# Keys and values as five tokens on each of 116 partitions: a fused cosformer attention and SwiGLU kernel

## The chip, the cores and the metric

The kernel runs on one core of one Trainium2 chip. The metric is device time in microseconds (us). Engines are called PE (TensorE; PEld is its weight load), DVE (VectorE), ACT (ScalarE), POOL (GpSimd) and SP (SyncE). SP computes nothing: it issues transfers, in its program's order. ACT and POOL issue transfers too. 16 DMA engines of the core carry them out.

## The reference

There are 8 batches, 8 heads, 576 tokens and a head size of 64. First linear attention, then a gated feed-forward layer on the 4,608 token rows of 512 numbers:

```python
r = np.maximum(x, 0.0)
phi(x) = np.concatenate([r * c, r * s], axis=-1)   # c, s: cos and sin of pi/2 * pos / S
kv = einsum('bhsf,bhsd->bhfd', phi(k), v);  z = sum(phi(k), axis=2)
num = einsum('bhsf,bhfd->bhsd', phi(q), kv)
den = einsum('bhsf,bhf->bhs', phi(q), z)[..., None] + 1e-06
x = num / den                                      # then the heads side by side: (4608, 512)
xn = x / sqrt(mean(x * x) + 1e-06) * rms_g
out = (silu(xn @ w_gate) * (xn @ w_val)) @ w_out   # 512 -> 1536 -> 512
```

All inputs and the output are float32. The sum over tokens in kv and z takes the tokens in any order, as long as k, v and the table of angles agree.

## The kernel before, in words

**Layout.** k and v of a batch are loaded into a tile `raw` of 128 partitions (line 77). Even heads lie on partitions 0 to 63, odd heads on 64 to 127; each partition holds nine consecutive tokens of its head (`kv_rows`, line 65; NC = 9), so one row piece is 9 x 64 x 4 = 2,304 bytes and a load has 128 x 4 pieces. `k_phi` (255) makes phi for one of the nine token slots `c`, all heads, one half (cos on DVE, sin on ACT): an instruction of 128 x 256 elements. `v_cast` (303) turns v to bf16 with a column of ones beside it, which gives z with kv. `kvz_pe` (312) multiplies: for each head pair, slot and half, a product over 64 rows, 72 in all per batch. For batch 0 the z sums (`z0_pe`, 324) and the kv sums (`kv0_pe`, 333) are made apart, since its v (`vv0`, cast by the load itself) comes later than k.

**After that, per batch:** the copy of the sums (`kvz_evac`, 343), eight products of 128 rows for each of four 128-token tiles (`nd_pe`, 347), the division (`nd_post`, 383), the norm (`x_sq`, `x_norm`), and a transpose that fills `xnT`, the moving operand of the feed-forward layer. Batches 0 and 1 are transposed by PE, later ones by transposes on the DMA engines issued from SP (`q_tr_dma` 278, `q_tails_tr_dma` 286, `x_tr_dma` 429).

**Blocks.** The feed-forward layer goes by blocks of 512 tokens, in the order 0, 1, 2, 3, 4, 5, 6, 8, 7; block 8 is the 64 last tokens of each batch ("tails"). A block has 12 steps of gate and value products (`gval_step`, 716) and four output tiles (`out_step`, 725; numbered 12 to 15). Attention work of the next batch is put between these steps by hand, in `slots`: `at(blk, n, where, f, ...)` (624) runs `f` in step n of block blk, "pe" before its matmuls, "pre" before the evaluation of its results, "post" after it. Every engine carries out its instructions in this written order.

**The order that the steps below touch.** For a batch nb from 2 on, processed in block b = nb - 1: k phi and v casts in steps 12 to 15 of block b - 1; q phi with its transposes in (b-1, 14), (b-1, 15), (b, 0), (b, 1); `kvz_pe` in step 2; `nd_pe` in steps 4, 6, 8, 10, the xn transposes one step later each. Block nb needs all of xnT before its first matmul. Loads of batch b + 2 are issued from SP in block b: k in step 0, v in step 3, q in step 6 (in block 1: 0, 5, 8). So SP's queue in a block reads: q transpose, k, q transpose, tail transpose, v, xn transpose, q, three xn transposes, then the output stores. The five `raw` buffers are a ring.

**Opening.** SP loads batch 0's k in two pieces (tokens 0 to 4 and 5 to 8 of each partition, lines 115, 116); ACT loads the gain `g4` (118); POOL issues q and v of batch 0, then the weights, batch 1's k and so on (157 to 175, 540 to 602). While k is on its way PE runs ten filler matmuls (505), DVE makes the table of angles (208 to 220) and splits the gain into three bf16 parts (`g_parts`, 183), which PE spreads over the partitions (`g_spread`, 196). Then phi of the nine slots (506 to 519), q, kv, and the first block in quarters as its inputs come (589 to 619).

**End.** The last output tile of block 7 is computed in two halves of 256 columns (728 to 734), so that the first is copied and stored while the second is computed.

Of the kernel before, what the change touches and what calls it, by code (L numbers as in the profile page):

```python
# [9 lines left out]
FP32 = mybir.dt.float32  # L10
# [7 lines left out]
def kernel(  # L18
# [18 lines left out]
    NC = S // 64  # L37
# [27 lines left out]
    def kv_rows(src, b, hps):  # L65
        return src[b, 2 * hps[0] : 2 * hps[1], :, :].rearrange(
            "(hp hh) (s c) d -> (hh s) hp (c d)", hh=2, c=NC
        )

# [5 lines left out]
    def raw_tile(which, b):  # L75
        if (which, b) not in raw:
            t = ring.tile([P, HP * NC * D], FP32, name="raw", tag="raw")
            raw[(which, b)] = t
        return raw[(which, b)]

    def raw_kv(which, b):
        return raw_tile(which, b)[:, :].rearrange("p (hp e) -> p hp e", hp=HP)
# [4 lines left out]
    def load_kv(which, b, hps=(0, HP), eng=nc.sync):  # L87
        src = k if which == "k" else v
        return eng.dma_start(
            out=raw_kv(which, b)[:, hps[0] : hps[1], :], in_=kv_rows(src, b, hps)  # L90
        )

    def load_q(b, js=(0, 4), eng=nc.sync):
        return eng.dma_start(
            out=raw_q(b)[:, :, js[0] * D : js[1] * D],
            in_=q_rows(b)[:, :, js[0] * D : js[1] * D],
        )
# [11 lines left out]
    def load_k_tokens(b, c0, c1):  # L109
        return nc.sync.dma_start(  # L110
            out=raw_kv("k", b)[:, :, c0 * D : c1 * D],
            in_=kv_rows(k, b, (0, HP))[:, :, c0 * D : c1 * D],
        )

    load_k_tokens(0, 0, 5)
    load_k_tokens(0, 5, NC)
    g4 = one.tile([4, P], FP32, name="g4")
    nc.scalar.dma_start(out=g4[:, :], in_=moe_rms_g.rearrange("(t p) -> t p", p=P))


    idx_i = one.tile([P, 14], mybir.dt.int32, name="idx_i")
    G.iota(idx_i[:, 0:9], pattern=[[1, 9]], base=0, channel_multiplier=9)
    G.iota(idx_i[:, 9:13], pattern=[[1, 4]], base=0, channel_multiplier=4)
    G.iota(idx_i[:, 13:14], pattern=[[0, 1]], base=512, channel_multiplier=1)
# [31 lines left out]
    vv0 = one.tile([P, HP, NC * D], BF16, name="vv0")  # L156
    load_q(0, (0, 2), G)
    for hp in range(0, HP, 2):
        G.dma_start(out=vv0[:, hp : hp + 2, :], in_=kv_rows(v, 0, (hp, hp + 2)))
    load_q(0, (2, 4), G)  # L160
    for n in range(0, NNT - 4, 4):
        load_w(wg, moe_w_gate, n, n + 4)
        load_w(wv, moe_w_val, n, n + 4)
# [13 lines left out]

    g3 = one.tile([4, 3, P], BF16, name="g3")
    gres = one.tile([4, 2, P], FP32, name="gres")
    sel = one.tile([4, NDT, P], BF16, name="sel")  # L180
    gb = one.tile([P, DM], FP32, name="gb")

    def g_parts():
        V.tensor_copy(
            out=sel[:, :, :], in_=ident[0:4, 0:4].unsqueeze(2).to_broadcast([4, NDT, P])
        )
        rest = g4
        for i in range(3):
            V.tensor_copy(out=g3[:, i, :], in_=rest[:, :])
            if i < 2:  # L190
                V.tensor_tensor(
                    out=gres[:, i, :], in0=rest[:, :], in1=g3[:, i, :], op=ALU.subtract
                )
                rest = gres[:, i, :]

    def g_spread(bank):
# [8 lines left out]
    fidx = one.tile([P, 14], FP32, name="fidx")  # L205
    th = one.tile([P, 28], FP32, name="th")
    tab = one.tile([P, 28], FP32, name="tab")
    V.tensor_copy(out=fidx[:, :], in_=idx_i[:, :])
    V.tensor_scalar(
        out=th[:, 0:14], in0=fidx[:, :], scalar1=ang, scalar2=None, op0=ALU.mult  # L210
    )
    for c0, c1, less in ((0, 9, 576.0), (13, 14, 64.0)):
        V.tensor_scalar(
            out=th[64:128, c0:c1], in0=fidx[64:128, c0:c1], scalar1=-less, scalar2=ang,
            op0=ALU.add, op1=ALU.mult,
        )
    V.tensor_scalar(
        out=th[:, 14:28], in0=th[:, 0:14], scalar1=math.pi / 2.0, scalar2=math.pi,
        op0=ALU.add, op1=ALU.min,
    )  # L220
    A.activation(out=tab[:, :], in_=th[:, :], func=AF.Sin)

# [3 lines left out]
    def cos_of(c):  # L226
        return tab[:, 14 + c : 15 + c]

    kp = one.tile([P, NC, HP, F], BF16, name="kp")
    vv = one.tile([P, HP, NC, E], BF16, name="vv")  # L230
# [24 lines left out]
    def k_phi(eng, b, c, part, hps=(0, HP)):  # L255
        o = slice(0, D) if part == 0 else slice(D, F)
        f = cos_of if part == 0 else sin_of
        src = raw_kv("k", b)[:, hps[0] : hps[1], c * D : (c + 1) * D]
        phi(eng, kp[:, c, hps[0] : hps[1], o], src, f(c))
# [8 lines left out]
    def q_phi(eng, b, j, part):  # L268
        o = slice(0, D) if part == 0 else slice(D, F)
        f = cos_of if part == 0 else sin_of  # L270
        phi(eng, qp_of((b, j))[:, :, o], raw_q(b)[:, :, j * D : (j + 1) * D], f(9 + j))

    def q_tails_phi(eng, pair, part):
        o = slice(0, D) if part == 0 else slice(D, F)
        f = cos_of if part == 0 else sin_of
        phi(eng, qp_of(("t", pair))[:, :, o], rqt[pair][:, :, :], f(13))
# [26 lines left out]
    def v_cast(eng, b, hps=(0, HP)):  # L303
        copy(
            eng, vv[:, hps[0] : hps[1], :, 0:D],
            raw_kv("v", b)[:, hps[0] : hps[1], :].rearrange("p hp (c d) -> p hp c d", d=D),
        )
# [4 lines left out]
    def kvz_pe(b, hps=range(HP)):  # L312
        for hp in hps:
            for c in range(NC):
                for g in range(2):
                    lo, hi = 64 * g, 64 * g + 64
                    nc.tensor.matmul(  # L317
                        heads[:, g, hp, :], lhsT=kp[lo:hi, c, hp, :], rhs=vv[lo:hi, hp, c, :],
                        start=(c == 0), stop=(c == NC - 1),
                    )  # L320
# [3 lines left out]
    def z0_pe(c):  # L324
        for hp in range(HP):
            for g in range(2):
                lo, hi = 64 * g, 64 * g + 64
                nc.tensor.matmul(
                    heads[:, g, hp, D:E], lhsT=kp[lo:hi, c, hp, :], rhs=ones[lo:hi, :],
                    start=(c == 0 and hp == 0), stop=False, skip_group_check=True,  # L330
                )

    def kv0_pe(hp):
        for c in range(NC):
            for g in range(2):
                lo, hi = 64 * g, 64 * g + 64
                nc.tensor.matmul(
                    heads[:, g, hp, 0:D], lhsT=kp[lo:hi, c, hp, :],
                    rhs=vv0[lo:hi, hp, c * D : (c + 1) * D],
                    start=False, stop=(hp == HP - 1 and c == NC - 1), skip_group_check=True,  # L340
                )
# [148 lines left out]
    def filler_k(c):  # L490
        for _ in range(2):
            nc.tensor.matmul(  # L492
                psC[1][:, 0 : HP * D], lhsT=warm[:, 0:P], rhs=kp[:, c, :, 0:D],
                start=True, stop=True,
            )
# [8 lines left out]
    g_parts()  # L504
    filler(10, psC[1])
    for c in range(NC):
        k_phi(V, 0, c, 0)
        if c < 7:
            k_phi(A, 0, c, 1)
        filler_k(c)  # L510
        if c == 3:
            g_spread(psC[0])
        if c == 6:
            for i in range(6):
                z0_pe(i)
    k_phi(V, 0, 7, 1)
    k_phi(V, 0, 8, 1)
    for i in range(6, NC):
        z0_pe(i)
# [111 lines left out]
    KCS = ((0, 1, 2), (3, 4), (5, 6), (7, 8))  # L631
    for c in range(NC):
        at(0, 4 + c // 3, "post", k_phi, V, 1, c, 0)
        at(0, 4 + c // 3, "post", k_phi, A, 1, c, 1)
# [6 lines left out]
    at(0, 8, "post", load_kv, "k", 2, (0, HP), G)  # L641
    at(0, 9, "post", v_cast, G, 1, (0, 2))
    at(0, 10, "pre", v_cast, V, 1, (2, 4))
    at(0, 10, "post", load_kv, "v", 2, (0, HP), G)
# [23 lines left out]
    for nb in range(2, B):  # L668
# [7 lines left out]
        for i in range(2):  # L676
            vb, vn = ((0, 15), (1, 0))[i] if first else (b - 1, 13 + 2 * i)
            at(vb, vn, "post", v_cast, V, nb, (2 * i, 2 * i + 2))
# [46 lines left out]
    def out_step(blk, j):  # L725
        n = 12 + j
        run(blk, n, "pe")
        if blk == last_blk and j == 3:
            for i, bank in enumerate((psC[1], psG[0])):
                cols = (256 * i, 256 * i + 256)  # L730
                for m in range(NNT):
                    out_mm(j, m, bank, cols)
                out_store(A if i == 0 else V, blk, j, bank, cols)
            return
        bank = psC[j % 2]
        for m in range(NNT):
            if m == NNT // 2:
                run(blk, n, "mid")
            out_mm(j, m, bank)
        run(blk, n, "pre")  # L740
        out_store(A, blk, j, bank)
        run(blk, n, "post")
# [40 lines left out]
```

## Time and profile before

| | |
|---|---|
| median of 3 runs | 326.97 us (326.74 to 327.19) |
| the profiled execution, device time | 327.27 us |
| its span, first to last instruction | 325.5 us |
| granted PE clock | 1.000 |
| PE, DVE, ACT, POOL busy | 97%, 56%, 52%, 12% of the span |
| HBM read, written | 37.75 MB, 9.44 MB |
| DMA queue of SP: packets, MB, share of 16 engines | 65,952, 39.73, 52.7% |
| DMA queue of POOL | 7,216, 13.17, 16.3% |
| k, v, q loads from SP: size, median time from issue to landing | 1152, 1152, 1024 KB: 7.2, 6.6, 8.5 us |
| batch 0's k, two pieces | 640 KB 5.0 us, 512 KB 6.0 us |
| q transposes, xn transposes | 24 and 24: 3.6 and 3.0 us to landing |
| phi of k: DVE, ACT, mean of one | 355 ns x74, 501 ns x70 |
| k-v products of 64 rows by 65 columns | 504 (seven batches) |

The page's first part gives each engine's busy share; its second cuts the span into 40 slices of 8.1 us, with busy tenths, and the bytes moved per second; its third lists the DMA queues. The chain is the work that ended last, followed back. A timeline row reads: start, duration, engine, line, operation, what is written and read, count, and in brackets the idle time ahead with its releaser; for SP it is the time of issue. A window row gives, for a stretch, busy times, the clock, the DMA engines' share and GB/s.

### The profile page before, as it was taken

The page shows a single profiled execution, that of the slowest core. Times are in us where ns is not written, and L with a number is a line of the kernel's source. Part 1 is how long each engine was busy: PE and PEld are TensorE (multiplying, and loading weights), DVE is VectorE, ACT ScalarE, POOL GpSimd, SP SyncE. Part 2 cuts the span into 40 slices and gives each one's busy share as a digit, 9 for nine tenths or more (in the row PEclk, how much of TensorE's full clock was granted, in tenths as well). Part 3 has the DMA queues.
Part 4 walks back from the last instruction along what each step waited for, and adds up shares of the span by engine and source line. Part 5 has one row for each costly group of instructions (what it writes and reads, how often), then busy time and mean ns, then how long its engine had stood idle before and what let it go on. Part 6 is the DMA issues. An engine that isn't in the chain of part 4 may idle for free.

```text
span 325.5 us, 6461 instructions
## 1 busy us (share of the span) xinstructions
PE 315.7 (97%) x2490; PEld 161.0 (49%) x2527; DVE 182.1 (56%) x390; ACT 169.4 (52%) x343; POOL 40.1 (12%) x76
## 2 busy tenths in 40 slices
PE   7999999999999999999999999999999999999995
PEld 3786555544454445444454445444544444444443
DVE  6676867567737783677557745782577034203410
ACT  4578637854675548546754575446644333223321
POOL 9680301001000100011001000110011000000000
PEclk9999999999999999999999999999999999999999
DMA  7999997889589978994699859964722300050002
GB/s 227 234 271 274 276 337 255 195 180 241 131 175 214 306 122 156 235 297 99 174 205 267 150 145 201 272 155 129 119 51 47 114 34 1 2 110 19 0 34 97
DMA packets 73207, 53.32 MB, mean 164 GB/s; under 512 B 50260, under 2 KB 61784, under 8 KB 73176
## 3 DMA queue, kind: packets, MB, share of 16 engines
q1 hardware_dynamic: 65952, 39.73, 52.7%
q0 software_dynamic: 7216, 13.17, 16.3%
q8 instruction: 20, 0.33, 0.4%
q14 instruction: 11, 0.09, 0.1%
q10 hardware_dynamic: 8, 0.00, 0.0%
HBM read 37.75 MB, written 9.44 MB: 145 GB/s over the span
## 4 chain that ended last, share of the span: by engine, by line
PE 86%; DMA 4%; DVE 4%; ACT 2%; issue 2%; DVEq 0%; ACTq 0%
PE psC L470 26%; PE psV L446 25%; PE psG L446 24%; PE psA L317 2%; PE psA L350 2%; DMA xnT<-xn 2%; DMA raw<-in_k_dram 2%; DVE xt L394 1%; DMA qpT<-qp 1%; DVE xn L416 1%; PE psG L569 1%; PE psV L569 1%; ACT scr L406 1%; PE psC L492 1%; PE psA L569 1%
## 5 line engine op out<-in xcount | busy, mean ns | idle before, releaser
L467 DVE TENSOR_TENSOR hT<-psV,sg 128x512 bf16<-128x512 f32 x104 | 71.6, 689 | 108.4 <-PE psV L446 67.3
L466 ACT ACTIVATE sg<-psG 128x512 f32<-128x512 f32 x104 | 61.5, 591 | 63.6 <-PE psG L446 54.9
L446 PE MATMUL psV<-xnT,wv 128*128 128x512 bf16 x361 | 93.9, 379 | 0.6
L470 PE MATMUL psC<-wo,hT 128*128 128x512 bf16 (+1 forms) x422 | 93.6, 376 | 0.5
L446 PE MATMUL psG<-xnT,wg 128*128 128x512 bf16 x352 | 92.3, 379 | 0.8 <-issue 0.3
L470 PEld LDWEIGHTS <-hT 128*128 128x128 bf16 x444 | 42.7, 98 | 47.3
L446 PEld LDWEIGHTS <-wv 128*128 128x128 bf16 x416 | 40.7, 98 | 49.1
L446 PEld LDWEIGHTS <-wg 128*128 128x128 bf16 x416 | 38.4, 98 | 41.7
L242 ACT COPY osb<-psC 128x512 f32<-128x512 f32 (+1 forms) x36 | 20.8, 579 | 49.9 <-PE psC L470 46.0
L411 POOL TENSOR_TENSOR rs<-ms,mhalf 128x1 f32<-128x1 f32 x36 | 19.8, 550 | 198.1 <-ACT scr L406 198.1
L406 ACT ACTIVATE scr<-xt 128x513 bf16<-128x513 f32 x36 | 22.9, 635 | 23.5 <-DVE xt L394 23.5
L248 ACT ACTIVATE kp<-raw,tab 128x256 bf16<-128x256 f32 x70 | 30.9, 501 | 3.3 <-DMA raw<-in_k_dram 3.3
L416 DVE SCALAR_TENSOR_TENSOR xn<-xt,rs,gb 128x512 bf16<-128x512 f32 x36 | 26.8, 744 | 10.0 <-POOL rs L411 10.0
L394 DVE TENSOR_TENSOR xt<-psA,rec 128x512 f32<-128x512 f32 x36 | 24.9, 691 | 1.2
L248 ACT ACTIVATE qp<-raw,tab 128x512 bf16<-128x512 f32 x32 | 22.6, 714 | 0.5 <-DMA raw<-in_q_dram 0.5
L250 DVE TENSOR_SCALAR kp<-raw,tab 128x256 bf16<-128x256 f32 x74 | 22.0, 355 | 1.3 <-DMA raw<-in_k_dram 1.3
L250 DVE TENSOR_SCALAR qp<-raw,tab 128x512 bf16<-128x512 f32 x31 | 15.1, 494 | 0.0
L350 PEld LDWEIGHTS <-qpT 128*128 128x128 bf16 x224 | 10.5, 97 | 7.1 <-issue 1.0
L446 PE MATMUL psV<-xnT_tail,wv 128*128 128x512 bf16 x48 | 12.3, 379 | 0.1
L446 PE MATMUL psG<-xnT_tail,wg 128*128 128x512 bf16 x46 | 12.0, 379 | 0.1
L350 PE MATMUL psA<-kvzs,qpT 128*128 128x65 bf16 x224 | 11.4, 193 | 0.5 <-DVE xt L394 0.5
L244 DVE CAST vv<-raw 128x1152 bf16<-128x1152 f32 x13 | 9.8, 754 | 0.0
(86 smaller groups left out, 147.9 us busy)
## 6 DMA issues: line engine op xcount, KB each, us to landing
out_dram<-osb SPq DMA_DIRECT2D x31, 256.0 KB, 2.3
raw<-in_k_dram SPq DMA_DIRECT2D x5, 1152.0 KB, 7.2
raw<-in_v_dram SPq DMA_DIRECT2D x5, 1152.0 KB, 6.6
raw<-in_q_dram SPq DMA_DIRECT2D x5, 1024.0 KB, 8.5
raw<-in_k_dram POOLq DMA_DIRECT2D x2, 1152.0 KB, 19.1
raw<-in_v_dram POOLq DMA_DIRECT2D x2, 1152.0 KB, 15.5
raw<-in_q_dram POOLq DMA_DIRECT2D x2, 1024.0 KB, 15.8
wg<-in_moe_w_gate_dram POOLq DMA_DIRECT2D x3, 512.0 KB, 13.9
```

The lines of the kernel that those rows point to most:

```text
L242: A.copy(out=o, in_=i)
L248: A.activation(out=out_ap, in_=in_ap, func=AF.Relu, scale=scale)
L250: eng.tensor_scalar(out=out_ap, in0=in_ap, scalar1=scale, scalar2=0.0, op0=ALU.mult, op1=ALU.max)
L350: nc.tensor.matmul(heads[:, g, hp, :], lhsT=qpT[:, h, j * P : (j + 1) * P], rhs=kvzs[b][:, g, hp * E : (hp + 1) * E], start=True, stop=True,)
L394: V.tensor_tensor(out=xt[:, 0:DM].rearrange("p (hp g d) -> p g hp d", g=2, d=D), in0=heads[:, :, :, 0:D], in1=rec[:, :, :].unsqueeze(3).to ...
L406: A.activation(out=scr[:, :], in_=xt[:, 0 : DM + 1], func=AF.Square, scale=1.0 / math.sqrt(DM), accum_out=ms[:, :],)
L411: G.tensor_tensor(out=rs[:, :], in0=ms[:, :], in1=mhalf[:, :], op=ALU.pow)
L416: V.scalar_tensor_tensor(out=xn[:, :], in0=x_of[(b, j)][:, 0:DM], scalar=rs_of[(b, j)][:, :], in1=gb[:, :], op0=ALU.mult, op1=ALU.mult,)
L446: nc.tensor.matmul(bank[:, cols[0] : cols[1]], lhsT=w[:, t, n * P : (n + 1) * P], rhs=x[:, t, cols[0] : cols[1]], start=(t == 0), stop=(t ...
L466: A.activation(out=sg[:, :], in_=g[:, 0:TB], func=AF.Silu)
L467: V.tensor_tensor(out=hT[:, n, :], in0=v[:, 0:TB], in1=sg[:, :], op=ALU.mult)
L470: nc.tensor.matmul(bank[:, 0 : cols[1] - cols[0]], lhsT=hT[:, n, j * P : (j + 1) * P], rhs=wo[:, n, cols[0] : cols[1]], start=(n == 0), st ...
```

## The change

k and v are no longer split into two halves by head. A partition holds five consecutive tokens of every head (NC = 5): row p has tokens 5p to 5p + 4, so 576 tokens take 116 rows, the last with one valid token. A load reads 116 rows with a step of 320 numbers, running on past a head's end into the next; for the last batch, where nothing follows, 115 rows are read and the 116th is filled by a load of its own with the last token. Slot 0 uses 116 rows, slots 1 to 4 use 115 (`rows_of`). Row pieces are 5 x 64 x 4 = 1,280 bytes, 116 x 8 per load.

With that: phi of k has five instructions of 512 columns per half instead of nine of 256; products go over 116 or 115 rows, one per head and slot, 40 per batch instead of 72; batch 0's k comes in four loads, slots 0 and 1 ahead of 2 to 4, heads 0 to 3 from SP and 4 to 7 from ACT; `g4` is loaded from SP behind them, and its split moves from DVE to POOL, ahead of the weight loads in POOL's order; the phi of k are dealt anew to steps 4 to 6 of block 0 and 12 to 15 later; the last output tile is computed in pieces of 256, 128 and 128 columns on three PSUM banks, copied by DVE, ACT and DVE.

```diff
-    NC = S // 64
+    NC = 5
+    KP = S // NC + 1
...
-    def kv_rows(src, b, hps):
-        return src[b, 2 * hps[0] : 2 * hps[1], :, :].rearrange(
-            "(hp hh) (s c) d -> (hh s) hp (c d)", hh=2, c=NC
-        )
+    def rows_of(c):
+        return KP if c == 0 else KP - 1
+
+    def kv_rows(src, b, hs=(0, H), cs=(0, NC)):
+        whole = src[b, hs[0] : hs[1], 0 : NC * (KP - 1), :].rearrange(
+            "h (p c) d -> p h (c d)", c=NC
+        )
+        part = whole[:, :, cs[0] * D : cs[1] * D]
+        if b == B - 1:
+            return part
+        return bass.AP(part.tensor, part.offset, [[NC * D, KP]] + list(part.ap)[1:])
...
+    def load_kv(which, b, eng=nc.sync, hs=(0, H), cs=(0, NC)):
         src = k if which == "k" else v
+        rows = KP - 1 if b == B - 1 else KP
+        eng.dma_start(
+            out=raw_kv(which, b)[0:rows, hs[0] : hs[1], cs[0] * D : cs[1] * D],
+            in_=kv_rows(src, b, hs, cs),
+        )
+        if rows < KP:
+            eng.dma_start(
+                out=raw_kv(which, b)[rows:KP, :, :].rearrange("p h (c d) -> p h c d", d=D),
+                in_=src[b, :, S - 1 : S, :].rearrange("h s d -> s h d").unsqueeze(2)
+                .to_broadcast([1, H, NC, D]),
+            )
...
-    load_k_tokens(0, 0, 5)
-    load_k_tokens(0, 5, NC)
+    for cs in ((0, 2), (2, NC)):
+        load_kv("k", 0, nc.sync, (0, 4), cs)
+        load_kv("k", 0, nc.scalar, (4, H), cs)
     g4 = one.tile([4, P], FP32, name="g4")
-    nc.scalar.dma_start(out=g4[:, :], in_=moe_rms_g.rearrange("(t p) -> t p", p=P))
+    nc.sync.dma_start(out=g4[:, :], in_=moe_rms_g.rearrange("(t p) -> t p", p=P))
...
+    def g_parts():
+        rest = g4
+        for i in range(3):
+            G.tensor_copy(out=g3[:, i, :], in_=rest[:, :])
+            if i < 2:
+                G.tensor_tensor(
+                    out=gres[:, i, :], in0=rest[:, :], in1=g3[:, i, :], op=ALU.subtract
+                )
+                rest = gres[:, i, :]
...
-    for hp in range(0, HP, 2):
-        G.dma_start(out=vv0[:, hp : hp + 2, :], in_=kv_rows(v, 0, (hp, hp + 2)))
+    for h in range(0, H, 4):
+        G.dma_start(out=vv0[0:KP, h : h + 4, :], in_=kv_rows(v, 0, (h, h + 4)))
     load_q(0, (2, 4), G)
+    g_parts()
     for n in range(0, NNT - 4, 4):
...
             for c in range(NC):
                 for g in range(2):
-                    lo, hi = 64 * g, 64 * g + 64
+                    h, r = 2 * hp + g, rows_of(c)
                     nc.tensor.matmul(
-                        heads[:, g, hp, :], lhsT=kp[lo:hi, c, hp, :], rhs=vv[lo:hi, hp, c, :],
+                        heads[:, g, hp, :], lhsT=kp[0:r, c, h, :], rhs=vv[0:r, h, c, :],
...
     for c in range(NC):
         k_phi(V, 0, c, 0)
-        if c < 7:
-            k_phi(A, 0, c, 1)
+        k_phi(A if c < 4 else V, 0, c, 1)
         filler_k(c)
+        if c == 2:
+            g_spread(psC[0])
         if c == 3:
-            g_spread(psC[0])
-        if c == 6:
-            for i in range(6):
+            for i in range(3):
                 z0_pe(i)
-    k_phi(V, 0, 7, 1)
-    k_phi(V, 0, 8, 1)
-    for i in range(6, NC):
+    for i in range(3, NC):
         z0_pe(i)
...
-    KCS = ((0, 1, 2), (3, 4), (5, 6), (7, 8))
+    KCS = ((0, 1), (2,), (3,), (4,))
...
-            for i, bank in enumerate((psC[1], psG[0])):
-                cols = (256 * i, 256 * i + 256)
+            pieces = ((V, psC[1], 0, 256), (A, psG[0], 256, 384), (V, psG[1], 384, 512))
+            for eng, bank, c0, c1 in pieces:
                 for m in range(NNT):
-                    out_mm(j, m, bank, cols)
-                out_store(A if i == 0 else V, blk, j, bank, cols)
+                    out_mm(j, m, bank, (c0, c1))
+                out_store(eng, blk, j, bank, (c0, c1))
```

Not shown: `z0_pe`, `kv0_pe` and the filler products, changed in the same way; the tables of angles, ten columns instead of fourteen; and the views of the tiles with eight heads instead of four head pairs.

## The prediction

> **What bounds the kernel now.** I read the page's shares first, then the chain, then the DMA rows, then SP's timeline.
>
> ```profile
> PE 315.7 (97%) x2490; PEld 161.0 (49%) x2527; DVE 182.1 (56%) x390; ACT 169.4 (52%) x343; POOL 40.1 (12%) x76
> DMA  7999997889589978994699859964722300050002
> GB/s 227 234 271 274 276 337 255 195 180 241 131 175 214 306 122 156 235 297 99 174 205 267 150 145 201 272 155 129 119 51 47 114 34 1 2 110 19 0 34 97
> PE 86%; DMA 4%; DVE 4%; ACT 2%; issue 2%; DVEq 0%; ACTq 0%
> ```
>
> TensorE sets the time, but the DMA row is the warning: up to slice 28 the 16 engines are 0.4 to 0.9 busy. The best slice moved 337 GB/s, 21.1 GB/s per engine; the window from 167 to 168 us shows 392, so 24.5. I price a busy engine at the middle, 22.8 GB/s (297 KB in 13.0 us), and keep 17.1 (274 GB/s between 5 and 13 us) as the slow end.
>
> Next, the chain in the opening and around one k-v product of block 4:
>
> ```profile
> 0.72 4.96 DMA raw<-in_k_dram
> 5.78 1.14 DVE kp L250 x3
> ...
> 158.36 0.86 PE psG L446 x4
> ...
> 161.82 1.27 PE psA L317 x72
> 163.08 0.32 PE psG L446
> ...
> 166.64 0.24 PE psA L350 x8
> ```
>
> The opening waits for batch 0's k. In block 4 TensorE runs without a gap: four matmuls of 512 columns take 0.86 us, and blocks follow at 33.9 us (158.36, then 192.27). So what TensorE does besides, or a load that is late there, moves the end.
>
> SP's queue in block 4 (issue times) and two rows on the queues:
>
> ```profile
> 163.44 1.38 SPq L89 DMA_DIRECT2D raw<-in_k_dram  x1
> 164.97 1.46 SPq L280 DMA_TRANSPOSE qpT<-qp  x1
> 167.97 2.73 SPq L289 DMA_TRANSPOSE qpTt<-qp  x1
> 170.74 0.58 SPq L89 DMA_DIRECT2D raw<-in_v_dram  x1
> 171.82 1.33 SPq L430 DMA_TRANSPOSE xnT<-xn  x1
> 173.20 0.58 SPq L94 DMA_DIRECT2D raw<-in_q_dram  x1
> 175.57 8.67 SPq L430 DMA_TRANSPOSE xnT<-xn  x3
> ...
> q10 hardware_dynamic: 8, 0.00, 0.0%
> raw<-in_k_dram SPq DMA_DIRECT2D x5, 1152.0 KB, 7.2
> ```
>
> The transposes that fill the next block's xnT stand on the same queue behind the k and v loads that this change reshapes.
>
> **The unknown that decides: how 116 rows are dealt to the engines.** The trace has no such load. The nearest rows: queue 10 carried one load, the gain, four rows in 8 packets, four rows and four closing packets, so four engines. On SP's queue, counted by row pieces (k and v 5,120, q 5,120, batch 0's k 1,024, q tails 4,096, stores 4,736, transposes 43,008 of 256 B), 65,952 - 63,104 = 2,848 packets remain: 16 for each of 122 issues and 16 more for each of 56 transposes. So loads of 128 and of 64 rows ran on 16 engines. Every load seen has equal shares per engine: 8, 4 or 1 rows. 116 rows make equal shares on 4 engines (29 each), not on 8 or 16. Bounds: 4 engines, or 16 with 7 or 8 rows each. I take 4, since no unequal share appears.
>
> The Trainium skill, page "DMA: Bandwidth & Descriptors", section on why a DMA increments its semaphore by 16, states the rule that speaks against this change: the generator takes the largest number up to 16 that divides the slowest dimension of both sides, and 100 partitions gave 10 engines. By it 116 rows get 4 engines and 115 rows 5; no run here shows it yet. The same section lets a GpSimd copy sometimes spread unevenly over all 16; by that exception the sum below would fall by some 12 us.
>
> **Part by part.**
>
> *Size of a load.* 116 rows x 8 heads x 1,280 B = 1,188 KB: 3.3 us on 16 engines at 22.8 GB/s, 13.0 us on four. For the ends of a load: batch 0's first (655 KB, 1.9 us of moving at 337 GB/s) landed 5.0 us after issue, so 3.1 us besides; I put 1.5 ahead and 1.5 behind (estimate).
>
> *Opening.* All four k loads (SP and ACT) meet on the same four engines: 297 KB each. POOL's q halves add 66 KB; one of the two v loads may fall on them as well (148 KB), I count half. 437 KB / 22.8 = 19.2 us; k is complete at 0.7 + 1.5 + 19.2 + 1.5 = 22.9 us (19.6 to 26.1). Two queues save issue time only if the engines are not the limit. After the last piece DVE owes four phi of 494 ns (its 128x512 row), 2.0 us: 24.9 instead of 9.46, **+15.4** (12 to 19). What hid the old load, ten filler matmuls that ended at 5.2 us, covers none of this.
>
> *The gain's parts move from DVE to POOL.* They free 2.0 us of DVE (2.41 to 4.45) that lay ahead of its wait for k: worth nothing. But the gain's load now stands on SP's queue behind k, and POOL waits for it before the weight loads. Five POOL ops are bounded by its memset (0.23) and cast (1.15); I take 0.4 each. Weights are issued from 22.9 + 2.8. POOL's queue moves a weight load in about 2.6 us (1.05 MB at 25 GB/s per engine); four of them, then batch 1's k on four engines (11.6), land at 22.9 + 2.8 + 1.5 + 10.4 + 11.6 + 1.5 = 50.7. Its first phi, at 28.57 before, is due at 44.0: 6.7 late, with DVE's and ACT's silu and hT work queued behind it. Batch 1's q follows two more weight loads, 2.1 late. **+8.8** (0, if POOL's loads use all engines, to 15).
>
> *Blocks 1 to 5.* From a block's start S, SP issues k at S + 5.1 (163.44 - 158.36). It moves from S + 6.6 to 19.6; the q transpose and the tail transpose behind it take 1.2 each (SP's rows 1.23); v leaves SP after them, 1.5 later, and moves from 23.5 to 36.5; the first xn transpose (half of q's bytes, 0.6), q (2.9), three xn transposes (1.8), 1.5 to land: S + 43.3 instead of a block of 33.9. Blocks 2, 3, 4: 9.4 each, 28.2. Block 1: k issued at 58.2, 59.7 to 72.7, four q transposes (4.8), v 79.0 to 92.0, then 0.6 + 2.9 + 1.8 + 1.5: 98.8 instead of 90.55, 8.3. Block 5 loads batch 7, 115 rows, equal on five engines: 10.3 a load and no tails, 36.7, 2.8. **+39.3.** At 24.5 GB/s a load takes 12.1 and the sum is about 32; at 17.1, 17.4 and about 83. Today the same chain has 3.5 us loads and ends near S + 26: that slack is the cover that goes.
>
> *k-v products.* 72 products of 64 rows take 1.27 us and delay the next by 0.11; 40 of 116 rows go by the nd row (eight of 128 rows, 0.24 us), 30 ns each, 1.20. That is -0.18 for seven batches, **-1.3**, paid out only where TensorE is the bound. In blocks 1 to 5 the wait for xnT swallows it; in batch 1 the wait for k does. Batch 0: 1.17 against 1.20; its z sums 1.07 against 0.6 to 1.2. I count 0, and keep -1.3.
>
> *DVE and ACT.* Nine phi of 256 columns become five of 512 (355 to 494 ns on DVE, 501 to 714 on ACT): about 0.7 and 0.9 us less per batch, both idle over 40%; nothing.
>
> *Last tile.* The last DVE copy shrinks from 0.42 to some 0.25 us, the last store by half: **-0.2**; one more issue on SP hides behind the matmuls.
>
> Sum: 15.4 + 8.8 + 39.3 - 0.2 = 63.3. Span 325.5 + 63.3 = 388.8; the profiled execution took 327.27, 1.77 around its span: 390.6, say **391 us**. That execution lies 0.3 above the median of the runs (326.97), less than my error.
>
> **Rivals.**
>
> *A: rows dealt over all 16 engines.* Then loads cost what they do now (1,188 against 1,180 KB). k's last piece still lands near 7.2; four phi end at 9.2 instead of 9.46, -0.3; products -1.3; last tile -0.2; against it the gain's detour, 0 to +0.8 on the gain's spread matmuls: -1.4, **325.9**, faster. For it: 64 and 128 rows do use 16. Against: never an unequal share. It decides from loads under about 8 us (the block's chain falls 2 us per us of load), seven engines or more, and only with batch 0's k complete by about 7 us.
>
> *B: four engines, but transposes do not stand behind the loads,* and prefetch a block ahead absorbs the rest: the opening alone, 24.2 - 0.2 gives 351.3. For it: the k issued at 163.44 is first read by a phi at 185.02. Against: the tail transpose holds SP for 2.73 us behind a k load, and even freely ordered, 26 us of loads plus the engines' other work (a DMA share of 0.87 over block 4's 33.9 us, less 7 for k and v: 22) exceed a block.
>
> **How the numbers follow.** Forecast, four engines and queue order: 0.78, own range 371 to 444 (12 to 19 for the opening, 0 to 15 behind POOL, 32 to 83 for the blocks). B: 0.10. A: 0.12, half of it faster, 0.05 within 0.2%, 0.01 slower if the gain's detour costs more. The range 345 to 440 takes in the forecast but its last few us, and B; it leaves out A and some of the forecast beyond its bounds: 0.8 remains. A measurement tells about 0.2% from no change. Faster 0.06, same 0.05, slower 0.89.
>
> **What would show it.** ACT's queue should show 4 closing packets per k load; the q, k and v rows' time to landing should rise from 7 to about 17 us for k and v and stay for q; the first kp phi should wait past 10 us; block starts should lie 40 us or more apart from block 1 to 4 with TensorE waiting for xnT<-xn; the last two blocks unchanged. Wrong if k lands in 7 us (A), or if blocks keep 33.9 us (B).

## The result and the profile after

The kernel after takes **423.72 us** (median of 6 runs, 416.9 to 429.23), the kernel before beside it 326.97 (median of 6). The ratio, 1.280 with an interval of 1.272 to 1.287, is formed from the three shorter executions (416.9 to 421.62 us, spans 415.1 to 419.8), while the profiled one, 427.94 us with a span of 426.1, is among the three longer. So the stages below add up to 100.6 us more span than before, 6 to 11 us more than in a shorter execution. The forecast was 391 us with a range of 345 to 440, and the measured time lies inside it: the sign and the main mechanism, four engines, held, and about a third of the loss was missing from the sum.

The page of the kernel after: busy shares, the 40 slices (now 10.7 us each), two of the DMA queues and the chain's shares.

```profile
PE 345.0 (81%) x2243; PEld 169.9 (40%) x2243; DVE 179.6 (42%) x352; ACT 166.4 (39%) x312; POOL 49.0 (11%) x81
...
PE   3149926798779579596959499868998999999997
...
PEclk8558986799689979799988979996999999999999
DMA  7559998775959889489497978499789613003002
...
q0 software_dynamic: 13104, 13.27, 19.1%
q10 hardware_dynamic: 936, 0.59, 0.5%
...
PE 41%; DMA 35%; issue 9%; DVE 7%; ACT 3%; POOL 2%; SPq 2%; ACTq 0%; DVEq 0%; POOLq 0%
```

PE's row has holes up to its 28th slice and hardly any behind it: where no k and v are loaded any more, the kernel runs as before. The chain, 86% PE before, is 35% DMA now. Queue 10 (ACT's) is the count that decides the prediction's unknown: ACT issues two k loads of 116 rows by 4 heads, 2 x 464 = 928 row pieces, and 936 - 928 = 8 packets are left, four closing packets for each load. The trace's packet records (start, duration and size of each packet) say the same of SP's loads: mostly four packets of a 116-row load are under way at once and five of batch 7's 115-row loads, where a 128-row load of the kernel before has mostly sixteen. **A load of 116 rows ran on four DMA engines.** In the PEclk row TensorE's granted clock, 9 throughout before, falls in and behind the holes of PE's row.

The opening (timeline; in brackets the idle time and its releaser):

```profile
15.94 1.33 ACT L262 ACTIVATE kp<-raw,tab 116x512 bf16<-116x512 f32 x2 [13.34 <-DMA raw<-in_k_dram]
24.53 0.28 POOL L178 CAST g<-g 4x128 bf16<-4x128 f32 x1 [17.77 <-DMA g<-in_moe_rms_g_dram]
26.90 1.90 DVE L264 TENSOR_SCALAR kp<-raw,tab 115x512 bf16<-115x512 f32 x4 [10.06 <-DMA raw<-in_k_dram]
42.13 1.05 PE L579 MATMUL psG<-xnT,wg 128*128 128x128 bf16 x16 [0.46 <-ACT xnT L256]
```

Batch 0's k is complete at 26.9 us, DVE's phi of it end at 28.8 (9.46 before), and the 2 KB of the gain, behind k on SP's queue, hold POOL until 24.5. The first gate product starts at 42.13 us; before, it was 18.87.

POOL's rows after that:

```profile
30.53 1.99 POOL L99 DMA_DIRECT2D raw<-in_k_dram  x1
...
63.26 1.99 POOL L99 DMA_DIRECT2D raw<-in_k_dram  x1 [15.62 <-issue]
82.62 1.90 POOL L258 CAST vv<-raw 116x1280 bf16<-116x1280 f32 x1 [17.36 <-DMA raw<-in_v_dram]
84.47 1.98 POOL L99 DMA_DIRECT2D raw<-in_v_dram  x1
```

POOL issues batch 1's k at 30.53, and its next k load (batch 2) stands still for 15.62 us until 63.26. In that time POOL waits for two semaphores, one of them that of batch 1's k load, which landed at 62.4. Batch 1's v lands at 82.6, and the v load of batch 2 can leave only behind its cast, at 84.47.

SP's queue in block 2 (issue times), the counterpart of the rows of block 4 above:

```profile
157.86 0.42 SPq L99 DMA_DIRECT2D raw<-in_k_dram  x1
158.45 13.69 SPq L295 DMA_TRANSPOSE qpT<-qp  x1
172.25 3.43 SPq L304 DMA_TRANSPOSE qpTt<-qp  x1
175.78 0.42 SPq L99 DMA_DIRECT2D raw<-in_v_dram  x1
176.29 10.35 SPq L443 DMA_TRANSPOSE xnT<-xn  x1
```

Before, the transpose behind a k load left SP's queue in 1.46 us. Now it needs 13.69, v follows only then, and the xn transpose behind v needs 10.35. The chain through two blocks shows what that does:

```profile
151.60 1.86 PE psG L459 x4
...
175.78 16.69 DMA raw<-in_v_dram
...
193.78 4.34 DMA xnT<-xn
...
204.07 17.98 DMA qpT<-qp
```

A v load takes 16.69 us on the chain; in the next block a q transpose takes 17.98. In the trace's packet records the k and v loads from SP move for 14.1 to 18.5 us each, 64 to 84 GB/s (batch 7's, with 115 rows, for 10.2 and 11.5). The first row is the clock's: four matmuls that take 0.86 us at full clock take 1.86 just after a wait, in a stretch (148.5 to 155.3 us) for which the trace records a granted clock of one half.

**Where the 100.6 us lie.** The lengths are those of the profiled execution. Starts of blocks are the first gate products of a block by the PE timeline.

| stage, length in us | before | after | more | forecast |
|---|---|---|---|---|
| opening and block 0 | 56.96 | 100.94 | +44.0 | +24.2 |
| block 1 | 33.43 | 50.66 | +17.2 | +8.3 |
| block 2 | 33.90 | 46.66 | +12.8 | +9.4 |
| block 3 | 33.91 | 47.67 | +13.8 | +9.4 |
| block 4 | 33.91 | 43.66 | +9.8 | +9.4 |
| block 5 | 33.42 | 37.51 | +4.1 | +2.8 |
| blocks 6, 8, 7 | 99.97 | 99.0 | -1.0 | -0.2 |

### The profile page after: what moved, and what is told of

Read it like the earlier page. It is cut to its first block, busy times and chain, and to the rows that moved or that the text cites. A ratio compares the mean times of both kernels' runs of the same rounds, so it can differ in the third digit from the quotient of the medians.

```text
span 426.1 us, 5869 instructions
## 1 busy us (share of the span) xinstructions
PE 345.0 (81%) x2243; PEld 169.9 (40%) x2243; DVE 179.6 (42%) x352; ACT 166.4 (39%) x312; POOL 49.0 (11%) x81
## 3 DMA queue, kind: packets, MB, share of 16 engines
q0 software_dynamic: 13104, 13.27, 19.1%
## 4 chain that ended last, share of the span: by engine, by line
PE 41%; DMA 35%; issue 9%; DVE 7%; ACT 3%; POOL 2%; SPq 2%; ACTq 0%; DVEq 0%; POOLq 0%
PE psG L459 14%; PE psV L459 14%; DMA raw<-in_v_dram 13%; PE psC L483 7%; DMA qpT<-qp 7%; DMA raw<-in_k_dram 6%; DMA xnT<-xn 5%; DMA raw<-in_q_dram 4%; DVE xn L429 3%; DVE xt L407 2%; PE psA L330 2%; ACT scr L419 2%; ACT sg L479 1%; POOL raw L99 1%; DVE kp L264 1%
## 5 line engine op out<-in xcount | busy, mean ns | idle before, releaser
L459 PE MATMUL psG<-xnT,wg 128*128 128x512 bf16 x368 | 106.1, 415 | 32.2 <-DMA xnT<-xn 23.9
L459 PE MATMUL psV<-xnT,wv 128*128 128x512 bf16 x368 | 102.5, 404 | 3.2 <-DVE hT L480 3.2
L459 PEld LDWEIGHTS <-wg 128*128 128x128 bf16 x416 | 40.7, 104 | 81.5 <-issue 40.3
L459 PEld LDWEIGHTS <-wv 128*128 128x128 bf16 x416 | 42.8, 103 | 59.7 <-issue 15.6
L262 ACT ACTIVATE kp<-raw,tab 115x512 bf16<-115x512 f32 (+1 forms) x39 | 27.0, 718 | 33.1 <-DMA raw<-in_k_dram 33.1
L256 ACT COPY osb<-psC 128x512 f32<-128x512 f32 x35 | 20.4, 582 | 49.2 <-PE psC L483 49.2
L262 ACT ACTIVATE qp<-raw,tab 128x512 bf16<-128x512 f32 x32 | 22.6, 713 | 29.9 <-DMA raw<-in_q_dram 29.9
L264 DVE TENSOR_SCALAR kp<-raw,tab 115x512 bf16<-115x512 f32 (+1 forms) x41 | 18.6, 488 | 32.8 <-DMA raw<-in_k_dram 32.8
L258 DVE CAST vv<-raw 116x1280 bf16<-116x1280 f32 x13 | 10.7, 826 | 32.5 <-DMA raw<-in_v_dram 32.5
L363 PE MATMUL psA<-kvzs,qpT 128*128 128x65 bf16 x224 | 12.0, 198 | 14.1 <-DMA qpT<-qp 13.6
L264 DVE TENSOR_SCALAR qp<-raw,tab 128x512 bf16<-128x512 f32 x31 | 14.8, 483 | 17.1 <-DMA raw<-in_q_dram 17.1
L506 PE MATMUL psC<-kp,warm 115*128 115x512 bf16 (+1 forms) x10 | 4.9, 615 | 20.3 <-DVE kp L264 20.3
L363 PEld LDWEIGHTS <-qpT 128*128 128x128 bf16 x224 | 10.7, 100 | 21.8 <-DMA qpT<-qp 15.6
L330 PE MATMUL psA<-vv,kp 116*128 116x65 bf16 (+1 forms) x280 | 10.8, 201 | 2.2 <-POOL vv L258 2.2
## 6 DMA issues: line engine op xcount, KB each, us to landing
wg<-in_moe_w_gate_dram POOLq DMA_DIRECT2D x3, 512.0 KB, 10.2
```

The source lines that it names most:

```text
L256: A.copy(out=o, in_=i)
L262: A.activation(out=out_ap, in_=in_ap, func=AF.Relu, scale=scale)
L264: eng.tensor_scalar(out=out_ap, in0=in_ap, scalar1=scale, scalar2=0.0, op0=ALU.mult, op1=ALU.max)
L363: nc.tensor.matmul(heads[:, g, hp, :], lhsT=qpT[:, h, j * P : (j + 1) * P], rhs=kvzs[b][:, g, hp * E : (hp + 1) * E], start=True, stop=True,)
L459: nc.tensor.matmul(bank[:, cols[0] : cols[1]], lhsT=w[:, t, n * P : (n + 1) * P], rhs=x[:, t, cols[0] : cols[1]], start=(t == 0), stop=(t ...
```

## The experiments

The theory: a load runs only on as many of the 16 engines as share its rows equally, 116 = 4 x 29 rows leave four, and the whole loss follows from that. Rivals: the wait is one of queue order (transposes behind loads), or of layout (five tokens, wider instructions). Each diff is against the kernel after, where it doesn't name another.

### 1. All loads of 116 rows in two pieces, 112 and 4

```diff
-        eng.dma_start(out=raw_kv(which, b)[0:rows, ...], in_=kv_rows(src, b, hs, cs))
+        for r0, r1 in ((0, 112), (112, rows)):
+            eng.dma_start(out=raw_kv(which, b)[r0:r1, ...], in_=kv_rows(src, b, hs, cs)[r0:r1])
```

and likewise batch 0's v. 112 divides by 16.

> The changed kernel with every load of 116 rows issued as two, 112 rows (equal shares on 16 engines) and the last 4 rows (for the last batch 112, 3 and the broadcast row); nothing else differs. Theory (the loads run on 4 engines, and what waits for them makes the whole loss): 324 to 327 us, block starts 31 to 34 us apart again, no wait of TensorE for xnT<-xn, SP's transposes not held over 5 us. Rival 1 (the pieces of 1,280 bytes, or the new order of work, are slow by themselves): over 390 us. Rival 2 (only part is the engines): between 335 and 390.

Measured: 333.24 us (5 runs, 332.39 to 334.0), ratio 1.0185 [1.0169, 1.0202]. Blocks 1 to 5 take 33.29, 33.78, 33.77, 33.76 and 33.29 us; block 1 starts at 63.55. So some 85 to 90 us of the loss go with the row count of the loads alone, the shape of tiles and products left as it is. Some 6 us stay, where 0 and less were expected, and all of them lie ahead of block 1.

### 2. The kernel before, its k and v loads in pieces of 124 and 4 rows

```diff
-        return eng.dma_start(out=raw_kv(which, b)[:, ...], in_=kv_rows(src, b, hps))
+        for r0, r1 in ((0, 124), (124, P)):
+            eng.dma_start(out=raw_kv(which, b)[r0:r1, ...], in_=kv_rows(src, b, hps)[r0:r1])
```

124 is 4 x 31. Batch 0's k and v are split in the same way.

> The kernel before with every k and v load issued as two, 124 rows (equal shares on 4 engines, 31 each) and 4 rows (4 engines); layout, products and order of work as before. Theory: 390 to 430 us, the loss of the change without the change, somewhat less than its 97 us since the gain's parts do not wait behind k. Rival 1 (the layout or the new order of work costs the time): 327 to 330 us.

Measured: 452.49 us (451.99 to 453.0), ratio 1.383. The loss comes without the change, and is even larger than foreseen: nine-token layout, old queues, old gain, only the row count differs. In the packet records mostly four packets of a 124-row load are under way at once. Together with the first experiment this excludes the layout as the main cause, and also the mere number of issues, since both kernels issue their k and v loads in two pieces.

### 3 and 4. The split for POOL's loads alone, and for SP's batches 3 to 7 alone

```diff
-        for r0, r1 in ((0, 112), (112, rows)):
+        for r0, r1 in ((0, 112), (112, rows)) if eng is nc.gpsimd else ((0, rows),):   # 3
+        for r0, r1 in ((0, 112), (112, rows)) if b >= 3 else ((0, rows),):             # 4
```

> The changed kernel with only POOL's loads of 116 rows (batch 0's v, k and v of batches 1 and 2) issued as 112 and 4 rows; batch 0's k and SP's loads of batches 3 to 7 as changed. Theory: block 1 starts at about 75 to 82 us instead of 100.9 (the wait for k, v of batches 1 and 2 goes, the one for batch 0's k stays), later blocks as in the changed kernel, 398 to 408 us. If POOL's loads already used more engines (as the uneven spread would have it): 415 to 430.

> The changed kernel with only SP's loads of batches 3 to 7 issued as 112 and 4 rows. Theory (queue order and occupancy of four engines in blocks 1 to 5): blocks 2 to 5 at 33 to 35 us each, block 1 between 34 and 45 since batch 2's v still lands late; 423 less some 50 to 57: 365 to 375 us. Rival B (transposes pass the loads, blocks lose little by them): over 400.

Measured: 399.51 us with block 1 at 78.76, and 377.51 us with block 1 at 98.97; both single runs. The third lies in its forecast, the fourth 2.5 us above it. PE's row of the fourth kernel (its slices are 9.4 us):

```profile
PE   4119891489929999999999999999999999999996
```

With SP's loads mended the holes end after the 12th slice: blocks 2 to 5 take 33.8, 33.8, 33.8 and 33.3 us. Together with the first experiment the spans divide the loss into four terms:

| term | from | us |
|---|---|---|
| batch 0's k on four engines | block 1's start, 78.76 - 63.55 | 15.2 |
| SP's k and v of batches 3 to 7 | span 397.7 - 330.6, less 15.2 | 51.9 |
| POOL's v of batch 0, k and v of batches 1 and 2 | span 426.1 - 397.7 | 28.4 |
| the rest of the change | span 330.6 - 325.5 | 5.1 |

They add up to 100.6 by construction. Taken in another order, SP's loads cost 50.4 (after less the fourth kernel), and POOL's 29.9 (fourth less first, less 15.2). But the third and fourth kernel ran once each, and executions of the kernel after differ by up to 12 us: against its shorter ones POOL's term would be 17 to 22. So a term is good to some 10 us. Of POOL's 28.4, 22.2 lie ahead of block 1.

### 5. All loads of 128 rows, the last 12 read and not used

```diff
-        return bass.AP(part.tensor, part.offset, [[NC * D, KP]] + list(part.ap)[1:])
+        return bass.AP(part.tensor, part.offset, [[NC * D, P]] + list(part.ap)[1:])
```

One load instead of two pieces, 10% more bytes (batch 7 keeps 112 and 3 rows).

> The changed kernel with every load of batches 0 to 6 reading 128 rows (rows 116 to 127 hold tokens of what follows and are never used), so equal shares on 16 engines in one issue; batch 7 as 112, 3 and the broadcast row. Theory for what the 112-row kernel still lost (its opening was 6.6 us longer than before: batch 0's k complete at 10.8 instead of 7.2, with eight issues on two queues and 4-row loads at their ends): k complete near 8.5, block 1 starts at 59 to 62, 328 to 331 us. Rival (the two queues share their engines with q and v as before, the number of issues does not matter): k complete at 10 to 11, block 1 at 63 to 64, 332 to 334.

Measured: 328.77 us, ratio 1.0048 [1.0036, 1.0061], block 1 at 60.04. As expected: batch 0's k is complete at 7.54 us instead of 10.81, and 3.5 of the 6.6 us are back that the first experiment had left ahead of block 1. Whether the extra issues or the four-row pieces cost them was not separated.

### 6 and 7. The gain back on ACT's queue and DVE, then batch 0's k from SP alone

```diff
+    nc.scalar.dma_start(out=g4[:, :], ...)          # 6, ahead of k; its split back on DVE (7 too)
     for cs in ((0, 2), (2, NC)):
-        load_kv("k", 0, nc.sync, (0, 4), cs)
-        load_kv("k", 0, nc.scalar, (4, H), cs)
+        load_kv("k", 0, nc.sync, (0, H), cs)        # 7 alone
```

> The 128-row kernel with the gain as in the kernel before: loaded first on ACT's queue, split by DVE while it waits for k, so that POOL issues the weights without a wait. Theory: the detour over POOL costs the opening 0 to 1.5 us (weights issued at 5.5 instead of 10.3, and the spread of the gain at once): block 1 starts 0 to 1.5 earlier than in the 128-row kernel. Rival: it costs nothing, within 0.3.

> As the kernel with 128 rows and the gain as before, and batch 0's k in two loads from SP alone (slots 0 and 1, then 2 to 4). Theory (two queues bring no bandwidth, only ACT's table and phi behind its issues): k complete at about 7.5, block 1 at 56 to 57.5, total 324.5 to 326.5, faster than before by the products (0.13 a block) and the last tile. Rival (two queues help): slower than with two queues by 1 us or more.

Measured: 332.23 us (ratio 1.0152 [1.0139, 1.0165]) and 327.63 us (1.0018 [1.0009, 1.0027]). Both missed. The sixth kernel is 3.5 us slower than the fifth, not faster: the gain's load ahead of k on ACT's queue puts ACT's k loads off (issued at 1.36 instead of 0.75), ACT's k phi begins at 6.42 instead of 5.13, and the clock records show TensorE at half speed up to 19.45 us instead of 15.12. In the seventh, DVE's k phi end at 9.55 us, level with before (9.46), and block 1 still starts 2.6 us late, at 59.57. Batch 0's k and its phi are therefore not what is left. The windows from 8 to 12 and from 12 to 16 us show what is, in their third column from the end (granted clock); the kernel before first, then the seventh:

```profile
8.00:12.00 4.00, 4.00 (x127) 3.26 (x126) 3.15 (x9) 2.47 (x5) 2.80 (x8) 1.00 1.15 261
12.00:16.00 4.00, 3.48 (x92) 2.40 (x86) 2.18 (x6) 2.54 (x5) 2.02 (x2) 1.00 1.24 209
```

```profile
8.00:12.00 4.00, 4.00 (x63) 2.71 (x62) 2.65 (x5) 2.43 (x5) 3.39 (x8) 0.69 1.29 233
12.00:16.00 4.00, 3.78 (x55) 3.72 (x55) 1.38 (x2) 0.34 (x1) 2.00 (x1) 0.50 1.19 229
```

TensorE is busy in both (4.00 of 4.00 us, then 3.48 and 3.78 of 4.00), but in the seventh its clock falls to 0.69 and 0.50 of full speed (the records have it at one half from 9.51 to 16.34 us), where before it stays at 1.00.

### 8. SP's batches 3 to 7 at 116 rows from ACT's queue, everything else in two pieces

```diff
-        at(b, 0, "post", load_kv, "k", nb)
+        at(b, 0, "post", load_kv, "k", nb, A)       # v likewise
```

> The 112-row kernel, but the k and v loads of batches 3 to 7 again as 116 rows (four engines), issued from ACT's queue and not from SP's, so that SP's transposes do not stand behind them in one queue. Theory (queue order makes the wait): blocks 1 to 5 at 34 to 38 us instead of the 45 us with SP's queue (block 1 start to block 6 start below 190 us instead of 220), total 340 to 355. Rival (the four engines are simply full, 26 us of loads beside 16 to 22 of other work): blocks at 42 to 46 us, total 375 to 392.

Measured: 398.79 us (one run); blocks 1 to 5 take 44.0, 47.8, 48.2, 47.0 and 45.7 us. The prediction explained the blocks by SP's queue order; this kernel takes that order away, and nothing is won; it is even a little slower than its rival forecast said. SP's and ACT's issue rows:

```profile
162.49 13.89 SPq L297 DMA_TRANSPOSE qpT<-qp  x3
```

```profile
158.66 0.26 ACTq L100 DMA_DIRECT2D raw<-in_k_dram  x1
```

No load stands ahead of the transposes on SP's queue any more, and three of them still need 13.89 us, with ACT's k load on its way since 158.66. In the packet records mostly four packets of these loads are under way at once, and k and v of a batch (3 to 6) move for 36 to 43 us together, longer than a whole block of the kernel before (33.9). So four engines are full whichever queue fills them. That the transposes wait for just these four is argued from this; the packet records don't name engines.

### 9 to 11. TensorE's speed in the opening

The seventh kernel with four, and with eight, more dummy matmuls in TensorE's idle time; and the kernel before with three dummy matmuls ahead of k phi instead of ten.

```diff
         filler_k(c)
+        if c == 1:
+            filler(4, psC[1])        # 9; filler(8, ...) in 10
```

```diff
-    filler(10, psC[1])
+    filler(3, psC[1])                # 11, in the kernel before
```

> As the 128-row kernel with k0 from SP alone (327.63 us, block 1 at 59.57 us, granted clock 0.50 from 10 to 16 us), with four more dummy matmuls of 512 columns behind the first two k phi columns, where TensorE stood idle for 0.89 us (6.94 to 7.83). Theory (what is left of the loss is TensorE's clock in the opening, halved because TensorE does little between 6.9 and 9.5 us): the granted clock stays at 1.00 up to 20 us, block 1 starts at 56.9 to 57.7, 324.7 to 325.9 us. Rival (the order of the work, wider k phi pieces and 116-row products cost the 2.6 us by themselves): clock or no clock, block 1 at 59 to 60, 327.2 to 328.4 us.

> The same with eight more dummy matmuls instead of four. At full clock eight of them take about 1.8 us (0.22 each, from the 256-column ones at 0.17 and 512-column ones at 0.34 with gaps, so 1.8 to 2.7), 0.9 to 1.8 of it beyond the idle time. Theory: the clock stays at 1.00 as with four or more surely than with four, block 1 at 57.5 to 58.7, 325.5 to 327 us. Rival: block 1 at 60 to 61.5, 328 to 330 us.

> The kernel before with 3 dummy matmuls ahead of its first k phi instead of 10, so that TensorE idles from about 2.6 to 6.2 us. Theory: the granted clock is halved in some stretch of the first 18 us, the opening's 2.6 us are lost without any change of loads, block 1 at 59 to 60.5 instead of 56.96, 329 to 330.5 us. Rival: the clock is 1.00 throughout or its loss lies beside other work, 326.5 to 327.3 us.

Measured: 327.65 us (ratio 1.0014 [1.0006, 1.0022], 12 runs), 327.57 (1.0010 [1.0001, 1.0019], 12 runs) and 331.07 (1.0108 [1.0092, 1.0124]).

The ninth has the clock back and its first gate product at 19.03 us (21.62 in the seventh, 18.87 before). That far the theory held. But block 1 starts at 58.96, not at 57, and the total is the rival's: a new wait has taken the place of the old one.

```profile
37.48 0.62 PE L312 MATMUL psC<-ident,qp 128*128 128x128 bf16 x8 [1.51 <-ACT qp L262]
```

ACT's q phi waited for batch 1's q, which landed at 36.68 us, 34.20 before. In the seventh kernel TensorE was late enough to meet it. The tenth is like the ninth: first gate product at 19.71, block 1 at 58.88. From block 1 to its end the ninth takes 266.9 us and the kernel before 268.5: the change wins 1.6 us there, and gives them back ahead of block 1.

The eleventh lost 3.9 us with no change of loads: dummy matmuls alone are worth that much here. The windows print a granted clock of 1.00 for it from 0 to 20 us, which looks as if the expected sign were missing. But the trace has no clock record ahead of TensorE's first change to full speed, and the view counts a stretch without a record as 1.00. The first record stands at 15.91 us in the eleventh kernel and at 4.52 in the kernel before. The durations agree with that; the kernel before first, then the eleventh:

```profile
1.18 3.97 PE L499 MATMUL psC<-warm 128*128 128x512 bf16 x10 [1.18 <-DVE ones L128]
6.22 1.38 PE L492 MATMUL psC<-kp,warm 128*128 128x256 bf16 x8 [1.08 <-DVE kp L250]
```

```profile
1.18 1.46 PE L499 MATMUL psC<-warm 128*128 128x512 bf16 x3 [1.18 <-DVE ones L128]
5.54 2.12 PE L492 MATMUL psC<-kp,warm 128*128 128x256 bf16 x8 [2.90 <-DVE kp L250]
```

In both kernels dummy matmuls of 512 columns start 0.427 us apart ahead of the first record and 0.216 us behind it. So TensorE did run at half speed, up to 15.91 us, as the theory had it.

### 12. Batch 1's q one place earlier on POOL's queue, in the ninth kernel

```diff
-    load_w(wv, moe_w_val, 8, NNT)
     load_q(1, eng=G)
+    load_w(wv, moe_w_val, 8, NNT)
```

> The 128-row kernel with four more dummy matmuls, and batch 1's q issued by POOL one place earlier, ahead of the last third of wv instead of behind it. In the kernel without this swap TensorE ran at full clock (first silu product at 19.03 us, 18.87 before) and still reached block 1 at 58.96 us (56.96 before), with 1.51 us of TensorE's wait at 37.48 on batch 1's q phi, whose q landed at 36.68 us (33.86 before). Theory (what is left is one late transfer, q, and the wv behind it has slack): q lands at 34 to 35.7, the wait at 37.5 goes, block 1 at 57.2 to 58.2, 325.9 to 327.0 us. Rival (the 16 DMA engines are full up to about 37 us and the 128-row loads move 320 KB more by then, so whichever load goes last is late): wv's last third lands at 35.5 to 37 instead, TensorE waits for it at 34.95 or for wg or v there, block 1 at 58.3 to 59.5, 327.1 to 328.2 us.

Measured: 327.46 us (12 runs), ratio 1.0006 [0.9996, 1.0016]: not to be told from before. Neither theory describes it. The wait for q is gone, as the first had it: q landed at 33.86, and from the first gate product to block 1 it takes 37.95 us (39.93 in the ninth, 38.09 before). The total and block 1, at 59.06, are the rival's, but TensorE shows no wait for wv. In the profiled execution, the longest of the twelve, the first gate product stands at 21.11 us: batch 0's k landed 0.57 us later than in the ninth, TensorE idled 0.73 us, its first clock record, the change to full speed, stands at 10.08 us instead of 5.53, and its four added dummy matmuls took 1.91 us instead of 1.03. Whether the later k comes from the swap, which issues nothing new ahead of it, or differs between executions, stays open. No version that beats the kernel before was found.

## Why the prediction was right in kind and too small

**Four engines: right.** Queue 10's eight closing packets, four packets under way at once, the first two experiments, and block lengths from 43.7 us on show it. Rival A (all 16) falls by the same rows. Batch 7's loads of 115 rows, for which the prediction took five engines, have mostly five packets under way and were hurt least (block 5, +4.1). The rule that the prediction cited from the Trainium skill, page "DMA: Bandwidth & Descriptors", section on why a DMA increments its semaphore by 16, agrees with this trace: four closing packets per load. Its exception for GpSimd, an uneven spread over 16, did not occur: in the packet records of POOL's queue four packets are under way while one of its 116-row loads of k and v moves, and about eight while two overlap (54 to 60 and 66 to 74 us). So such a load had four engines, and two that overlap did not share the same four.

**Opening, +15.4: the mechanism right, the size too small.** The sum took it as the delay of DVE's last phi of batch 0's k: 28.8 instead of 9.46 us, so +19.3, just beyond its bound of 19. k was complete at 26.9, 4.0 later than worked out and 0.8 beyond its bound of 26.1. The 15.2 us of the table above are nearer to the forecast, but are counted from the first experiment's kernel, which loses 6.6 us of its own ahead of block 1; that nearness is luck.

**Behind POOL, +8.8 (0 to 15): the step that failed.** Measured: 28.4, good to some 10 us, of which 22.2 ahead of block 1. Two things were wrong. Batch 1's k was given 11.6 us of moving at 25 GB/s per engine; its packets begin at 38.87 and it landed at 62.4, 23.5 us, at some 14 GB/s per engine (55 GB/s from 39 to 53 us) beside weights and q on POOL's queue. So it landed 11.7 us after the 50.7 of the sum. And the sum followed batch 1's k and q and stopped there. It left out POOL's other loads of 116 rows: batch 1's v landed at 82.6, and batch 2's k waited at POOL for batch 1's k to land, so its v left at 84.47 and landed at 107.2 (22.70 on the chain), in the first part of block 1. That each load adds a wait to a later issue on its own queue is a row of the trace after; nothing in the sum asked for it.

**Blocks 1 to 5, +39.3: the wait foreseen, its reason only in part, the size too small.** 50.4 to 51.9 for SP's loads. The load was priced at 13.0 us and took 14.1 to 18.5; with the prediction's own slow end, 17.1 GB/s per engine and 83 us, the term would have been too large. Two of the waits that the prediction said would be seen:

```profile
DVE kp L264 <- DMA raw<-in_k_dram: 32.8, 3, 13.6
...
PE psG L459 <- DMA xnT<-xn: 23.9, 5, 6.8
```

The first row's three waits lie ahead of block 1: twice for batch 0's k, once for batch 1's. The second is TensorE's wait at the starts of blocks 2 to 6 (23.9 us in five waits). But the reason given, that transposes stand *behind* the loads on SP's queue, falls with experiment 8: with the loads on another queue the blocks are no shorter. What is left is the occupancy of four engines. That the size came as near as it did is luck in part. Rival B (no queue order, so the opening only) had the right thought about the queue and the wrong price.

**A term that was missing: TensorE's speed after a wait.** The mean granted clock of the execution is 0.896. The windows from 60 to 70, 150 to 200 and 300 to 330 us:

```profile
60.00:70.00 10.00, 5.72 (x14) 1.97 (x14) 4.27 (x8) 4.61 (x8) 1.99 (x1) 0.50 0.92 158
...
150.00:200.00 50.00, 40.02 (x241) 18.36 (x242) 21.86 (x44) 19.96 (x39) 2.74 (x5) 0.88 0.84 140
...
300.00:330.00 30.00, 28.70 (x162) 13.40 (x160) 17.78 (x36) 15.73 (x31) 2.19 (x4) 1.00 0.96 185
```

Such a wait is paid twice, once while it lasts and once in slow matmuls behind it. The sum took every matmul at the duration of the trace before. PE is busy for 345.0 us here and for 318.2 in the first experiment with the same products, so the slow matmuls add some 27 us of busy time. How many of the missing 37 us are this could not be separated, since part of the 27 passes beside other waits and no run kept the waits and the clock apart.

**Products, counted 0 (-1.3 where TensorE is the bound): small as said.** In the first experiment, whose blocks have no wait, they are 33.78 long instead of 33.91: -0.13 per batch against -0.18 forecast.

**Last tile, -0.2: somewhat more.** From block 7's first gate product to the end it takes 34.3 us in the first experiment, 34.98 before: -0.7, with the products that this stretch doesn't have. The three pieces were not tried alone.

**The opening's rest, counted 0: +5.1 between the profiled executions, 6.0 between the medians.** Of the 6.0, single 128-row loads take back 4.5 (333.24 to 328.77), the gain and k as before another 1.1. What remains, 0.46 us between the medians of the seventh kernel and of the kernel before beside it (327.63, 327.17), lies in the opening: with TensorE at full speed it meets the late q, with q earlier it is level. Whether Rival A's 325.9 would have come true with 116 rows on 16 engines no run shows. The nearest kernels, with 128-row loads, did not reach it; their loads carry 10% more bytes into a stretch in which the DMA engines are 0.9 busy or more (8 to 57 us in the ninth kernel's slices).

## What to carry to other kernels

Before a tile's partition count is changed, count on how many DMA engines the load then runs: 116 rows on four engines cost 97 us here, the same data in pieces of 112 and 4 rows 6, in rows padded to 128 less than 2. A load that holds four engines for 15 us delays every transfer that needs them, on any queue, so price it by what else is on those engines, and follow every later issue on its queue. A wait on TensorE is to be priced with the slow matmuls behind it, and a granted clock is to be read only where the trace has a record of it.

## What was not expected of the hardware

- **A printed clock of 1.00 where no clock was recorded.** In the kernel before and in the seventh and the ninth to twelfth TensorE starts slow: dummy matmuls of 512 columns start 0.427 us apart. The first clock record stands where that ends, at 4.06 to 6.10 us, but at 10.08 in the twelfth and 15.91 in the eleventh kernel, and ahead of it the windows print 1.00. The Trainium skill, page "TensorE: Matmul & The Clock Gate", Part 1, gives 426.7 ns cold for 512 columns, and these rows agree. It also warns that such clock records can be unreliable; here they fit the durations, and only the value printed ahead of the first record misleads. Durations are the surer sign.
- **POOL's issue of a 116-row load takes longer**, 1.99 us instead of 0.76, and its queue carries 13,104 packets instead of 7,216 for about the same bytes.
- **A dummy matmul can be worth its time.** Seven fewer of them ahead of the first k cost the kernel before 3.9 us, with the change to full speed 11.4 us later.
